# An attention and mixture-of-experts kernel: tile 0 head pair by head pair, two more value buffers, and 14 result tiles held on chip

## The chip, the cores and the metric

One NeuronCore of a Trainium2 chip. The metric is device time of one execution in microseconds (us), as the median of several runs. Matrix products run on TensorE (PE), row reductions and most element-wise work on VectorE (DVE), exponentials and scaled copies on ScalarE (ACT), a few copies and all gathers and scatters on GpSimd (POOL); the plain DMA transfers are issued by SyncE (SP), in program order.

## The reference

Two layers, one after the other, in float32.

1. Attention: q, k, v of shape 4 x 8 x 768 x 64 (batch, heads, sequence, width). Each query attends to the keys nearer than 16 positions and, beside them, to 24 summary keys: the maxima of k over blocks of 32 positions, with log(32) added to the scaled score; the summary values are the means of v over those blocks. One softmax goes over both parts.
2. Mixture of experts: the attention result as 3072 rows of 512. Noisy gates choose two of 8 experts for a row; each chosen expert gives relu(x w1) w2 (512 to 1024 to 512), weighted by the softmax of the two gate values, and the two are added.

## The kernel before

**Attention.** The 3072 rows are 24 tiles of 128 queries, 6 tiles a batch. Heads are held in 4 pairs (`HP`). A tile has 96 local and 24 summary keys for each half of 64 queries. For tile t the work is: `mask_sums` (mask into PSUM), `scores` (32 products), `smax` (row maxima on VectorE), `sexp` (8 exponentials on ScalarE), `p_trans` (8 transposes, copied out by ScalarE), `av` (32 products with the values, into the one PSUM buffer "o"), `norm` (VectorE divides by the sums and writes the result tile X[t]; this empties "o"), `x_pe` and `x_copy` (transpose for the gates), and `x_out` (one DMA of 256 KB writes X[t] to the scratch array `xd` in memory, from where the experts gather rows).

**Order.** It is written out by hand. A loop over steps t = -2 .. 22 issues in step t: the query load of tile t + 5, `norm` of tile t - 1, mask and scores of tile t + 2, its maxima, the transposes of tile t + 1, the exponentials of tile t + 2, the products with the values of tile t, then the transposes of tile t - 1, the second value load of tile t + 3 (`v_load`) and the write of tile t - 2. `at(t, f)` hangs extra pieces into a step: `run(t + 0.1)` and the like call them at fixed places of step t. Each engine runs its own part of this order strictly in sequence, so a piece that waits holds up what stands behind it on its engine.

**Keys.** `KB` holds the keys of a batch (two buffers); `KX` (three buffers) holds for a tile the local keys and the 24 maxima (`kx_local`, `kx_sum`). For batch 0 the keys come as four loads, one a head pair, and `k_head` takes the maxima; for later batches `load_k` brings three tiles' keys (768 KB) and `k_piece` takes the maxima on VectorE, for batch 1 in steps 1 to 3 (two pieces a step), for batch 2 from step 3 on.

**Values.** `VE` holds 128 rows of values a tile, `VD` the 96 rows that its second half of queries needs: three buffers a batch parity, used in turn, so `v_load(3)` waits until tile 0 has been multiplied. Rows 96 to 119 of `VE` and 0 to 23 of `VD` are the 24 block means, from `v_sums` (48 products, four VectorE copies, then GpSimd copies) and `v_rest` (a DMA for the remaining tiles).

**Start.** 100 products of the identity (`warm_up`, line 246) run on TensorE while the first loads come. The loads are queued as: query tile 0, the four key heads, query tile 1, six value tiles, query tile 2, further value and query tiles, gate weights and noise, query tile 4, then batch 1's keys in steps -1 and 0.

**Result tiles.** X[t] has five buffers; tile t is written to `xd` in step t + 2. In step 20 the tokens of tiles 0 to 11 that go to expert 0 are gathered from `xd` (`x_gather`, line 791).

**Experts.** After the attention come the 8 experts in order of their load, mostly dense products on TensorE (lines 854, 909, 1357, 1429), with gathers and scatters on GpSimd. Their buffers for expert 0 (the weights `WT[0]`, the transposed tokens `XTE[0]`) are not in use before step 20, apart from the w1 halves.

Of the kernel before, what the change touches and what calls it, by code (L numbers as in the profile page):

```python
# [8 lines left out]
F32 = mybir.dt.float32  # L9
# [5 lines left out]
OP = mybir.AluOpType  # L15
# [24 lines left out]
QN = 3  # L40
QBUF = 5
QA = 5
WARM = 100
SK = HP * NK
SW = 16 * (D + 1)
NCH = 7
# [17 lines left out]
def attn_moe(ctx, tc, qt, kt, vt, wgn, noise, w1, w2, out):  # L64
# [44 lines left out]
    def load_q(t):  # L109
        QR[t] = QT[t % QBUF]  # L110
        b, j = divmod(t, TS)
        nc.sync.dma_start(QR[t].rearrange("p h b q -> p (h b q)"), qt[b, j])

    def kx_local(t):
        b, j = divmod(t, TS)
        k = KB[b % 2][:, :, j * P:j * P + 64 + W]
        n = HP // 2 if t < 1 else HP
        for h in range(0, HP, n):
            for blk in range(2):
                x, y = KX[t % QN][:, h:h + n, blk, L0[blk]:L0[blk] + W], k[:, h:h + n, 64 * blk:64 * blk + W]  # L120
                if t < 2:
                    nc.scalar.activation(x, y, AF.Copy)
                else:
                    nc.gpsimd.tensor_copy(x, y)

    def kx_sum(t):
        b, j = divmod(t, TS)
        if j < QN:
            x = KX[t % QN].rearrange("p h b k -> p h (b k)")[:, :, W:W + 2 * NB]
            (nc.gpsimd if b else nc.vector).tensor_copy(x.rearrange("p h (b n) -> p h b n", b=2),  # L130
                                                        KM[b][:, :, None, :].to_broadcast([P, HP, 2, NB]))

    def q_piece(t):
        kx_local(t)
        kx_sum(t)

    flat = [x.rearrange("p f n -> p (f n)").bitcast(F32) for x in HT]
    VE = [flat[0][:, :TS * VB].rearrange("p (j c) -> p j c", j=TS), keep.tile([P, TS, VB], F32, name="ve")]
    VD = [[flat[1][:, VB * j:VB * (j + 1)] for j in range(3)],
          [keep.tile([P, VB], F32, name=f"vd{j}") for j in range(2)] + [flat[1][:, 3 * VB:4 * VB]]]  # L140

    def load_ve(b, j):
        nc.sync.dma_start(VE[b % 2][:, j].rearrange("p (h d) -> p h d", h=H), vt[b, j * P:(j + 1) * P])

    load_q(0)
    for h in range(HP):
        nc.sync.dma_start(KB[0][:, h, PAD:PAD + S], kt[0, :, h])


    ji = HT[1].rearrange("p f n -> p (f n)").bitcast(I32)[:, SW:SW + P]  # L150
    nc.gpsimd.iota(ji, pattern=[[1, P]], base=0, channel_multiplier=-1)
# [82 lines left out]
    def k_head(h):  # L234
        if h == 0:
            KM[0] = work.tile([P, HP, NB], F32, name="kmax")
        nc.vector.tensor_reduce(KM[0][:, h], KB[0][:, h, PAD:PAD + S].rearrange("p (n i) -> p n i", i=BLK),
                                axis=AX.X, op=OP.max)

    VO = []  # L240

# [8 lines left out]
    def v_sums(b):  # L250
        if b:
            pt = psum.tile([P, HP, P], F32, name="pt", bufs=2).rearrange("p a b -> p (a b)")
        else:
            pt = psum.tile([P, 2, 512], F32, name="o")[:, 0]
        for j in range(TS):
            for g in range(4):
                nc.tensor.matmul(pt[32 * g:32 * g + NB, 0:C4], ind[:, j, :], VE[b % 2][:, j, C4 * g:C4 * g + C4],
                                 start=(j == 0), stop=(j == TS - 1), skip_group_check=True)
        x, y = VE[b % 2][W:W + NB], [z[0:NB] for z in VD[b % 2]]
        for g in range(4):  # L260
            i, o = pt[32 * g:32 * g + NB, 0:C4], slice(C4 * g, C4 * g + C4)
            if b == 3 and g % 2:
                nc.scalar.activation(x[:, 0, o], i, AF.Copy)
            elif b:
                nc.vector.tensor_copy(x[:, 0, o], i)
            else:
                nc.vector.tensor_copy(x[:, 0, o], i)
        if b == 1:
            nc.gpsimd.tensor_copy(y[0], x[:, 0])
        if b == 0:  # L270
            for i in range(4):
                if i:
                    nc.gpsimd.tensor_copy(x[:, i], x[:, 0])
                if i < 3:
                    nc.gpsimd.tensor_copy(y[i], x[:, 0])

    def v_rest(b):
        x = VE[b % 2][W:W + NB]
        j = 1 if b else 4
        nc.sync.dma_start(x[:, j:], x[:, 0, None, :].to_broadcast([NB, TS - j, VB]))  # L280
        if b:
            for y in VD[b % 2][b == 1:]:
                nc.sync.dma_start(y[0:NB], x[:, 0])

    VX = {}

    def v_load(t):
        b, j = divmod(t, TS)
        y = VD[b % 2][j % 3].rearrange("p (h d) -> p h d", h=H)
        nc.sync.dma_start(y[NB:NB + VR], vt[b, P * j + 64:P * j + 64 + VR])  # L290
        VX[t] = [VE[b % 2][:, j].rearrange("p (h d) -> p h d", h=H), y]

# [16 lines left out]
                                 m[r, None, :].to_broadcast([64, HP, W]), start=True, stop=False,  # L309
                                 skip_group_check=True)  # L310

    def scores(t):
        s, q, k = SC[t], QR[t], KX[t % QN]
        for hp in range(HP):
            for blk in range(2):
                for a in range(2):
                    d = slice(64 * a, 64 * a + 64)
                    nc.tensor.matmul(s[64 * blk:64 * blk + 64, a, hp, :], q[d, hp, blk], k[d, hp, blk, :], start=False,  # L318
                                     stop=hp == HP - 1, skip_group_check=True)
# [16 lines left out]
    def p_trans(t, a):  # L336
        pt = psum.tile([P, HP, P], F32, name="pt", bufs=2)
        for hp in range(HP):
            if t == 0:
                warm_up(1 if a + hp else 8)  # L340
            nc.tensor.transpose(pt[:NK, hp, :], PE_[t][:, a, hp, :], ident)  # L341
        if a == 0:
            PT[t] = awork.tile([P, 2, HP, P], F32, name="pts")
        nc.scalar.activation(PT[t][:NK, a], pt[:NK], AF.Copy)
# [11 lines left out]
                                 start=True, stop=True, skip_group_check=True)  # L356

    xd_w = []

    def norm(t, fill=None):  # L360
        o = PO[t][:, :, :4 * (D + 1)].rearrange("p g (h c) -> p g h c", c=D + 1)
        r = work.tile([P, 2, 4], F32, name="r")
        nc.vector.tensor_scalar(r, o[:, :, :, D], 1e-9, 1.0 / XS, op0=OP.add, op1=OP.mult)
        if fill:
            fill()
        ri = work.tile([P, 2, 4], F32, name="ri")
        nc.vector.reciprocal(ri, r)
        X[t] = work.tile([P, DM], F32, name="x", bufs=5)
        nc.vector.tensor_tensor(X[t].rearrange("p (g h c) -> p g h c", g=2, h=4), o[:, :, :, 0:D],
                                ri[:, :, :, None].to_broadcast([P, 2, 4, D]), op=OP.mult)  # L370

# [419 lines left out]
    def x_gather(e, c, rows=N):  # L791
        if c >= chunks(e):
            return
        if c == 0 and e != 1:
            XTE[e] = (late[0] if e % 2 else moe).tile([P, 2 * DC, CAP], F16, name="xte")
        n = min(P, CAPS[e] - c * P)
        x = XG[gi[0] % len(XG)]
        gi[0] += 1
        r = indirect(
            out=x[:n].bitcast(F32), out_offset=None, in_=xd[:rows],  # L800
            in_offset=bass.IndirectOffsetOnAxis(ap=tb_of(e, c)[:n, 0:1], axis=0),
            bounds_check=rows - 1, oob_is_err=False)
        XC[e, c] = x
        return r
# [162 lines left out]

    warm_up(WARM)
    load_q(1)
    for j in range(TS):  # L970
        load_ve(0, j)
    load_q(2)
    v_load(0)
    v_load(1)
    load_q(3)
    v_load(2)
    nc.sync.dma_start(wg32, wgn)
    nc.sync.dma_start(noi, noise)
    load_q(4)
    for h in range(HP):  # L980
        k_head(h)
    q_piece(0)
    q_piece(1)
    at(-0.9, v_sums, 0)
    at(0.8, v_rest, 0)

    w_alloc(0)
    W0 = [8, 10, 12, 14]
    for i in range(4):
        at(W0[i], w_load, 0, i)  # L990
# [69 lines left out]
    for t in range(-2, NT - 1):  # L1060
        if QBUF <= t + QA < NT:
            load_q(t + QA)
        u = t + 3
        if t >= 1:
            norm(t - 1, (lambda: kx_sum(u)) if u < NT and u != TS else None)
        run(t + 0.02)
        run(t + 0.03)
        if t + 2 < NT:
            mask_sums(t + 2)
            scores(t + 2)  # L1070
        if t == -1:
            q_piece(2)
            q_piece(3)
        run(t + 0.5)
        if t + 2 < NT:
            smax(t + 2)
        if 0 <= t + 1 < NT:
            p_trans(t + 1, 0)
            p_trans(t + 1, 1)
        if t + 2 < NT:  # L1080
            sexp(t + 2, (0, 1) if t + 3 < NT else (0,))
        if u < NT and t >= 1:
            kx_local(u)
        run(t + 0.1)
        if u == TS:
            kx_sum(u)
        run(t + 0.2)
        if t >= 0:
            av_space(t)
        if t + 3 == NT:  # L1090
            sexp(t + 2, (1,))
        if t >= 0:
            av(t)
        run(t + 0.3)
        run(t + 0.31)
        if t >= 1:
            x_pe(t - 1)
        run(t + 0.4)
        if t >= 1:
            x_copy(t - 1)  # L1100
        run(t)
        run(t + 0.8)
        run(t + 0.9)
        if 0 <= t and t + 3 < NT:
            v_load(t + 3)
        if t >= 2:
            x_out(t - 2)

    norm(NT - 2)
# [594 lines left out]
```

## Time and profile before

| | |
|---|---|
| median of 3 runs | 644.94 us (644.83 to 646.68) |
| span of the profiled execution (first to last instruction) | 642.7 us |
| its own time beside the span | not listed apart; the median is 2.24 us above the span |
| TensorE busy | 621.8 us (97%) |
| VectorE, ScalarE, GpSimd busy | 481.6, 316.0, 249.0 us |
| moved by DMA | 127.91 MB, mean 199 GB/s |
| attention stage | about the first 131 us |

The profile is one execution. Its views: the page (busy shares, the span in 40 slices, the costliest groups), the chain of work that ended last, waits by engine, timelines of one engine, and a table by stretches. A releaser "issue" means that the engine waited for nothing that the profile shows.

### The profile page before, as it was taken

The numbers are of one execution on the slowest core, as the hardware profiler recorded it, in microseconds if no ns is written. First come the engines' busy times: TensorE is split into PE (matmuls) and PEld (weight loads), VectorE is DVE, ScalarE is ACT, GpSimd is POOL, SyncE is SP. The second block draws the span as 40 slices with busy tenths as digits, with TensorE's granted clock in tenths as the row PEclk, the third lists the DMA queues.
The fourth block names the chain that finished last, engine by engine and source line by source line (L and its number), as shares of the span: only waits on it lengthen the run. The fifth ranks groups of instructions, "written<-read, shape, count | busy, mean of one in ns | idle before, by whom it ended". The sixth has DMA issues, their size and how long they took to land.

```text
span 642.7 us, 14142 instructions
## 1 busy us (share of the span) xinstructions
PE 621.8 (97%) x5295; PEld 360.3 (56%) x5295; DVE 481.6 (75%) x1039; ACT 316.0 (49%) x692; POOL 249.0 (39%) x432
## 2 busy tenths in 40 slices
PE   8899899899999999999999999999999999999995
PEld 7678777765554554555455544554554455445542
DVE  5848899889797599178878887987898679757510
ACT  4958898852153463065337534654464255425300
POOL 4433044203254433623573256336632542333041
PEclk9989999999999999999999999999999999999999
DMA  9999996678469696636986688779786868763021
GB/s 308 296 294 327 296 303 211 214 265 288 139 200 187 188 221 152 256 91 162 203 245 162 150 212 261 169 139 220 220 199 157 217 202 165 180 193 120 3 95 50
DMA packets 123707, 127.91 MB, mean 199 GB/s; under 512 B 83242, under 2 KB 86674, under 8 KB 123630
## 3 DMA queue, kind: packets, MB, share of 16 engines
q1 hardware_dynamic: 111838, 90.66, 52.9%
q0 software_dynamic: 11792, 36.27, 17.9%
q8 instruction: 43, 0.70, 0.4%
q14 instruction: 34, 0.28, 0.1%
HBM read 81.85 MB, written 25.61 MB: 167 GB/s over the span
## 4 chain that ended last, share of the span: by engine, by line
PE 78%; DVE 11%; ACT 3%; issue 3%; DMA 3%; POOL 0%; POOLq 0%; SPq 0%; DVEq 0%; ACTq 0%
PE pt L1429 29%; PE h L1357 16%; PE h L854 8%; PE pt L909 7%; PE pt L1357 3%; PE o L1357 3%; PE h L909 2%; DVE nm L325 2%; DMA htl<-in_vt_dram 2%; ACT p L333 2%; PE pt L341 1%; PE o L354 1%; PE o L246 1%; PE s L318 1%; DVE y L920 1%
## 5 line engine op out<-in xcount | busy, mean ns | idle before, releaser
L90 POOL DMA_INDIRECT out_dram<-y,tb x52 | 69.3, 1333 | 167.5 <-DVE y L931 129.3
L90 POOL DMA_INDIRECT xg<-xd,tb x54 | 60.4, 1119 | 118.9 <-DVE dsc L653 32.9
L1429 PEld LDWEIGHTS <-hth 128*128 128x128 f16 x576 | 56.4, 98 | 66.7
L931 DVE SCALAR_TENSOR_TENSOR y<-pt,tb,prev 128x512 f32<-128x512 f32 x42 | 31.5, 749 | 65.7 <-PE pt L1429 54.2
L1357 PEld LDWEIGHTS <-w1h 128*128 128x128 f16 x504 | 48.9, 98 | 38.1 <-issue 4.1
L1429 PE MATMUL pt<-w2h,hth 128*128 128x512 f16 x288 | 69.0, 379 | 0.0
L1429 PE MATMUL pt<-w2l,hth 128*128 128x512 f16 x288 | 69.0, 379 | 0.0
L1429 PE MATMUL pt<-w2h,htl 128*128 128x512 f16 x288 | 69.0, 379 | 0.0
L1357 PEld LDWEIGHTS <-w1l 128*128 128x128 f16 x504 | 49.3, 98 | 34.9
L90 POOL DMA_INDIRECT prev<-out_dram,tb x45 | 52.1, 1158 | 24.6 <-issue 12.9
L333 ACT ACTIVATE p<-s,nm 128x120 f32<-128x120 f32 x192 | 50.8, 376 | 0.8
L854 PE MATMUL h<-xte,w1h 128*128 128x384 f16 (+2 forms) x248 | 48.9, 336 | 0.0
L1429 PEld LDWEIGHTS <-htl 128*128 128x128 f16 x288 | 28.2, 98 | 34.0
L1346 ACT ACTIVATE w1h<-stg 128x768 f16<-128x768 f32 (+1 forms) x24 | 22.7, 944 | 40.2 <-DVE stg L1337 40.2
L1389 ACT ACTIVATE hth<-h 128x384 f16<-128x384 f32 (+4 forms) x48 | 23.8, 496 | 35.6 <-PE h L1357 35.6
L1346 ACT ACTIVATE w1l<-stg 128x768 f16<-128x768 f32 (+1 forms) x24 | 22.5, 942 | 37.3 <-DVE stg L1337 37.3
L1357 PE MATMUL h<-xte,w1h 128*128 128x384 f16 (+4 forms) x180 | 39.7, 329 | 0.7 <-DVE h L1383 0.4
L1357 PE MATMUL h<-xte,w1l 128*128 128x384 f16 (+4 forms) x180 | 39.7, 329 | 0.0
L1310 ACT ACTIVATE x<-xt 128x512 f16<-128x512 f32 (+2 forms) x44 | 26.5, 626 | 23.2 <-issue 19.1
L1337 DVE TENSOR_TENSOR stg<-stg 128x256 f32<-128x256 f32 x96 | 36.3, 419 | 0.8
L854 PEld LDWEIGHTS <-w1h 128*128 128x128 f16 x256 | 24.7, 98 | 19.4 <-issue 1.0
L1392 DVE SCALAR_TENSOR_TENSOR htl<-h,hth 128x384 f16<-128x384 f32 (+4 forms) x48 | 26.4, 563 | 11.8 <-ACT hth L1389 11.5
(301 smaller groups left out, 1297.3 us busy)
## 6 DMA issues: line engine op xcount, KB each, us to landing
stg<-in_w_dram SPq DMA_DIRECT2D x64, 512.0 KB
q<-in_qt_dram SPq DMA_DIRECT2D x24, 256.0 KB
xd<-x SPq DMA_DIRECT2D x24, 256.0 KB
out_dram<-xg SPq DMA_DIRECT2D x8, 768.0 KB
kb<-in_kt_dram SPq DMA_DIRECT2D x6, 768.0 KB
hth<-in_vt_dram SPq DMA_DIRECT2D x12, 260.0 KB
htl<-in_vt_dram SPq DMA_DIRECT2D x16, 195.0 KB
ve<-in_vt_dram SPq DMA_DIRECT2D x12, 260.0 KB
```

The lines of the kernel that those rows point to most:

```text
L90: return nc.gpsimd.indirect_dma_start(**kw)
L333: nc.scalar.activation(PE_[t][:, a, hp, :], SC[t][:, a, hp, :], AF.Exp, bias=NM[t][:, 1, a, hp:hp + 1], scale=0.125)
L854: nc.tensor.matmul(ph[:, :n], w1_of(w, wn, c, f), x[:, xo + c, c0:c1], start=(k == 0), stop=(k == 11))
L909: nc.tensor.matmul(py, hx[:, f, c * P:c * P + P], wv[:, f, :], start=st, stop=sp)
L931: nc.vector.scalar_tensor_tensor(y, py[:, :d], gw, pv[:, :d], op0=OP.mult, op1=OP.add)
L1310: nc.scalar.activation(t[:r, c:c + k], src, AF.Copy)
L1337: nc.vector.tensor_tensor(o, x, y, op=op)
L1346: nc.scalar.activation(hi, x, AF.Copy, scale=W1S)
L1357: nc.tensor.matmul(ph[:, :h], w[:, la, a, P * j:P * j + P], x[:, j, :h], start=start and k == 0, stop=k == 5, skip_group_check=True)
L1389: nc.scalar.activation(hh[:, f, t], src, AF.Relu)
L1392: nc.vector.scalar_tensor_tensor(hl[:, f, t], src, 0.0, hh[:, f, t], op0=OP.max, op1=OP.subtract)
L1429: nc.tensor.matmul(py, x, wv[:, f, :], start=st, stop=sp, skip_group_check=True)
```

## The change

- The keys of batch 0 are loaded as heads 0 and 1, query tile 0, head 2, and head 3 in two halves. Tile 0 is worked head pair by head pair (`start`): maxima of the keys and their copy, local keys on ScalarE, scores, 6 warm-up products after each of the first three, then the row maximum and the two exponentials of the head pair before. `WARM` falls from 100 to 48, the 15 warm-up products among tile 0's transposes go, and 12 stand in step 0 after the scores. Local keys of tile 1 move from ScalarE to GpSimd, and the copies of the maxima of tiles 1 and 2 from VectorE to GpSimd.
- `v_sums(0)` moves from step -1 to step 0, behind tile 1's transposes and ahead of tile 0's products with the values. Query tile 2 is loaded ahead of the value tiles.
- Batch 0's second value tile has five buffers (batch 2 still uses three of them); `v_load(3)` and `v_load(4)` are issued in the first queue, behind query tile 4, and no longer in steps 0 and 1. `v_sums(0)` has two more GpSimd copies.
- The result tiles 0 to 13 are written into expert 0's buffers (four in w2h, four in w2l, six in XTE[0]), and their DMAs to `xd` are issued in steps 13 to 19, two a step. Tiles 14 on are written as before.

```diff
-WARM = 100
+WARM = 48
...
-    VD = [[flat[1][:, VB * j:VB * (j + 1)] for j in range(3)],
+    VD = [[flat[1][:, VB * j:VB * (j + 1)] for j in (0, 1, 2, 4, 5)],
...
+    VN = (5, 3, 3, 3)
...
-    load_q(0)
     for h in range(HP):
-        nc.sync.dma_start(KB[0][:, h, PAD:PAD + S], kt[0, :, h])
+        if h == 2:
+            load_q(0)
+        for c in ((0, S // 2), (S // 2, S)) if h == HP - 1 else ((0, S),):
+            nc.sync.dma_start(KB[0][:, h, PAD + c[0]:PAD + c[1]], kt[0, :, h, c[0]:c[1]])
...
+    def start_head(h):
+        k_head(h)
+        for blk in range(2):
+            nc.scalar.activation(KX[0][:, h, blk, L0[blk]:L0[blk] + W], KB[0][:, h, 64 * blk:64 * blk + W], AF.Copy)
+        if h == 0:
+            mask_sums(0)
+        scores(0, h, h + 1)
+        if h < HP - 1:
+            warm_up(6)
+        if h:
+            start_max(h - 1)
+
+    def start_max(h):
+        nc.vector.tensor_reduce(NM[0][:, 0, :, h], SC[0][:, :, h], axis=AX.X, op=OP.max)
+        nc.scalar.activation(NM[0][:, 1, :, h], NM[0][:, 0, :, h], AF.Copy, scale=-0.125)
+        for a in range(2):
+            nc.scalar.activation(PE_[0][:, a, h, :], SC[0][:, a, h, :], AF.Exp, bias=NM[0][:, 1, a, h:h + 1],
+                                 scale=0.125)
...
-        y = VD[b % 2][j % 3].rearrange("p (h d) -> p h d", h=H)
+        y = VD[b % 2][j % VN[b]].rearrange("p (h d) -> p h d", h=H)
...
-            if t == 0:
-                warm_up(1 if a + hp else 8)
...
-        X[t] = work.tile([P, DM], F32, name="x", bufs=5)
+        X[t] = XS_[t] if t < len(XS_) else work.tile([P, DM], F32, name="x", bufs=5)
...
     load_q(1)
+    load_q(2)
     for j in range(TS):
         load_ve(0, j)
-    load_q(2)
     v_load(0)
+    load_q(3)
     v_load(1)
-    load_q(3)
     v_load(2)
     nc.sync.dma_start(wg32, wgn)
     nc.sync.dma_start(noi, noise)
     load_q(4)
...
+    v_load(3)
+    v_load(4)
+    at(0.1, v_sums, 0)
     at(0.8, v_rest, 0)
...
+    XTE[0] = moe.tile([P, 2 * DC, CAP], F16, name="xte")
+    for x in (WT[0]["w2h"], WT[0]["w2l"], XTE[0]):
+        x = x.rearrange("p a b -> p (a b)").bitcast(F32)
+        for i in range(x.shape[1] // DM):
+            XS_.append(x[:, DM * i:DM * i + DM])
+    for t in range(len(XS_)):
+        at(13 + t // 2, lambda t: x_out(t), t)
...
+        if t == 0:
+            warm_up(12)
...
-        if 0 <= t and t + 3 < NT:
+        if 0 <= t < NT - 3 and t + 3 > 4:
             v_load(t + 3)
-        if t >= 2:
+        if t - 2 >= len(XS_):
             x_out(t - 2)
```

## Rows read from the trace of the kernel before

**Rows 1.** Table by stretches: busy time of PE, PEld, DVE, ACT, POOL, clock, DMA, GB/s

```profile
16.00:30.00 14.00, 13.69 (x282) 11.17 (x278) 11.09 (x22) 12.94 (x43) 6.44 (x12) 1.00 1.01 300
30.00:37.00 7.00, 4.75 (x74) 4.06 (x75) 3.72 (x9) 3.21 (x11) 1.53 (x4) 0.76 1.06 284
64.00:92.00 28.00, 25.75 (x527) 20.74 (x519) 25.20 (x84) 24.09 (x78) 8.57 (x14) 1.00 1.00 316
92.00:120.00 28.00, 25.49 (x556) 21.09 (x560) 26.59 (x96) 24.47 (x77) 7.34 (x14) 1.00 0.61 190
```

**Rows 2.** Chain of waits, first 62 us: start, us, what

```profile
21.79 10.41 DMA htl<-in_vt_dram
32.25 1.93 PE o L354 x30
...
36.61 1.02 PE pt L341 x8
37.63 1.08 PE o L354 x32
...
39.30 1.46 PE pt L257 x48
...
41.05 0.82 PE s L318 x32
...
42.35 0.90 issue
...
44.00 1.08 PE o L354 x32
```

**Rows 3.** Timeline of SP's queue, 19 to 41 us: start, us, what it issues

```profile
19.07 1.29 SPq L107 DMA_DIRECT2D kb<-in_kt_dram  x2
...
27.33 0.33 SPq L290 DMA_DIRECT2D htl<-in_vt_dram  x1
30.97 0.34 SPq L112 DMA_DIRECT2D q<-in_qt_dram  x1
...
32.43 0.56 SPq L290 DMA_DIRECT2D htl<-in_vt_dram  x1
...
40.87 1.27 SPq L290 DMA_DIRECT2D vd<-in_vt_dram  x1
```

**Rows 4.** Timelines of VectorE and GpSimd, 27 to 32 us

```profile
27.29 0.69 DVE L231 TENSOR_REDUCE kmax<-kb 128x16 f32<-128x512 f32 x1 [1.26 <-DMA kb<-in_kt_dram]
...
28.93 1.15 DVE L325 TENSOR_REDUCE nm<-s 128x8 f32<-128x960 f32 x1
29.99 2.46 DVE L231 TENSOR_REDUCE kmax<-kb 128x16 f32<-128x512 f32 x4
...
31.32 0.64 POOL L130 COPY kx<-kmax 128x192 f32<-128x192 f32 x2 [7.22 <-DVE kmax L231]
```

**Rows 5.** Timeline of all engines, 6 to 18 us: tile 0

```profile
6.09 2.91 DVE L237 TENSOR_REDUCE kmax<-kb 128x24 f32<-128x768 f32 x3 [0.39 <-DMA kb<-in_kt_dram]
...
11.96 2.12 ACT L333 ACTIVATE p<-s,nm 128x120 f32<-128x120 f32 x8
...
14.39 1.53 PE L257 MATMUL o<-hth 128*24 128x130 f32 x48
...
15.99 1.21 DVE L267 COPY hth<-o 24x130 f32<-24x130 f32 x4 [3.07 <-PE o L257]
...
17.32 0.62 POOL L275 COPY htl<-hth 24x520 f32<-24x520 f32 x1 [5.79 <-issue]
```

**Rows 6.** Line 246 (warm-up), 1.5 to 4.5 us and 6 to 9 us: ns min/median/max

```profile
L246 PE MATMUL o<-identb x28: 289/314/314, 1.5 to 4.4; 128*128 128x128 bf16 x28
...
L246 PE MATMUL o<-identb x53: 219/219/219, 5.8 to 8.7; 128*128 128x128 bf16 x53
```

**Rows 7.** Chain of waits, 62 to 140 us

```profile
66.33 1.63 issue
```

More of the change, by code (lines that the diff above doesn't have):

```diff
@@ L116, in kx_local @@
         k = KB[b % 2][:, :, j * P:j * P + 64 + W]
[L117 to L124, printed above, removed]
+        for blk in range(2):
+            nc.gpsimd.tensor_copy(KX[t % QN][:, :, blk, L0[blk]:L0[blk] + W], k[:, :, 64 * blk:64 * blk + W])
     def kx_sum(t):
@@ L129, in kx_sum @@
             x = KX[t % QN].rearrange("p h b k -> p h (b k)")[:, :, W:W + 2 * NB]
-            (nc.gpsimd if b else nc.vector).tensor_copy(x.rearrange("p h (b n) -> p h b n", b=2),
+            (nc.gpsimd if t else nc.vector).tensor_copy(x.rearrange("p h (b n) -> p h b n", b=2),
                                                         KM[b][:, :, None, :].to_broadcast([P, HP, 2, NB]))
@@ L236, in k_head, with start @@
             KM[0] = work.tile([P, HP, NB], F32, name="kmax")
-        nc.vector.tensor_reduce(KM[0][:, h], KB[0][:, h, PAD:PAD + S].rearrange("p (n i) -> p n i", i=BLK),
-                                axis=AX.X, op=OP.max)
+        for n in ((0, NB // 2), (NB // 2, NB)) if h == HP - 1 else ((0, NB),):
+            nc.vector.tensor_reduce(
+                KM[0][:, h, n[0]:n[1]],
+                KB[0][:, h, PAD + BLK * n[0]:PAD + BLK * n[1]].rearrange("p (n i) -> p n i", i=BLK),
+                axis=AX.X, op=OP.max)
+        x = KX[0][:, h].rearrange("p b k -> p (b k)")[:, W:W + 2 * NB]
+        nc.vector.tensor_copy(x.rearrange("p (b n) -> p b n", b=2), KM[0][:, h, None, :].to_broadcast([P, 2, NB]))
+    def start_head(h):
+        k_head(h)
+        for blk in range(2):
+            nc.scalar.activation(KX[0][:, h, blk, L0[blk]:L0[blk] + W], KB[0][:, h, 64 * blk:64 * blk + W], AF.Copy)
[12 more added lines that the diff above has]
+                                 scale=0.125)
+    def start():
+        NM[0] = work.tile([P, 2, 2, HP], F32, name="nm", bufs=2)
+        PE_[0] = awork.tile([P, 2, HP, NK], F32, name="p")
+        for h in range(HP):
+            start_head(h)
+        start_max(HP - 1)
+        q_piece(1)
     VO = []
@@ L258, in v_sums @@
                                  start=(j == 0), stop=(j == TS - 1), skip_group_check=True)
-        x, y = VE[b % 2][W:W + NB], [z[0:NB] for z in VD[b % 2]]
+        x, y = VE[b % 2][W:W + NB], [z[0:NB] for z in VD[b % 2][:VN[b]]]
         for g in range(4):
@@ L270, in v_sums @@
         if b == 0:
-            for i in range(4):
-                if i:
+            for i in range(VN[0]):
+                if 0 < i < 4:
                     nc.gpsimd.tensor_copy(x[:, i], x[:, 0])
-                if i < 3:
-                    nc.gpsimd.tensor_copy(y[i], x[:, 0])
+                nc.gpsimd.tensor_copy(y[i], x[:, 0])
     def v_rest(b):
@@ L281, in v_rest @@
         if b:
-            for y in VD[b % 2][b == 1:]:
+            for y in VD[b % 2][b == 1:VN[b]]:
                 nc.sync.dma_start(y[0:NB], x[:, 0])
@@ L310, in mask_sums, with scores @@
                                  skip_group_check=True)
-    def scores(t):
+    def scores(t, h0=0, h1=HP):
         s, q, k = SC[t], QR[t], KX[t % QN]
-        for hp in range(HP):
+        for hp in range(h0, h1):
             for blk in range(2):
@@ L358, in attn_moe @@
     xd_w = []
+    XS_ = []
     def norm(t, fill=None):
@@ L793, in x_gather @@
             return
-        if c == 0 and e != 1:
+        if c == 0 and e > 1:
             XTE[e] = (late[0] if e % 2 else moe).tile([P, 2 * DC, CAP], F16, name="xte")
@@ L979, in attn_moe @@
     load_q(4)
[L980 to L984, printed above, removed]
+    v_load(3)
+    v_load(4)
+    at(0.1, v_sums, 0)
     at(0.8, v_rest, 0)
     w_alloc(0)
+    XTE[0] = moe.tile([P, 2 * DC, CAP], F16, name="xte")
[5 more added lines that the diff above has]
+        at(13 + t // 2, lambda t: x_out(t), t)
     W0 = [8, 10, 12, 14]
@@ L1067, in attn_moe @@
         run(t + 0.03)
-        if t + 2 < NT:
+        if t == -2:
+            start()
+        elif t + 2 < NT:
             mask_sums(t + 2)
@@ L1074, in attn_moe @@
         run(t + 0.5)
-        if t + 2 < NT:
+        if t == 0:
+            warm_up(12)
+        if -2 < t < NT - 2:
             smax(t + 2)
@@ L1079, in attn_moe @@
             p_trans(t + 1, 1)
-        if t + 2 < NT:
+        if -2 < t < NT - 2:
             sexp(t + 2, (0, 1) if t + 3 < NT else (0,))
```

## The prediction

> **What bounds the kernel now.** I read the slices of the page first: TensorE is busy nearly everywhere, but the DMA row shows full tenths for the first 92 us only. The table by stretches says the same in numbers: from 16 to 30 us and from 64 to 92 us the DMA engines are full (share 1.01 and 1.00) at 300 and 316 GB/s, from 92 to 120 us they are at 0.61 [rows 1]. So I read the chain of waits of the first 62 us next. It is TensorE work except for one long piece: a value load ("htl") issued at 21.79 us that lands 10.41 us later, at 32.2 [rows 2]. That is the second value tile of tile 3. It is asked for only when tile 0 has left its buffer (three buffers), and by then it queues behind a dozen others. TensorE waits for it 2.28 us, and then the granted clock falls: the mean from 30 to 37 us is 0.76 [rows 1], and the 30 products of tile 3 take 1.93 us where a whole set of 32 takes 1.08 [rows 2].
>
> The SP queue shows why it lands so late. At most eight transfers are on their way: one is issued when the eighth before it has landed. Two loads show it: the value load at 27.33 follows the landing of the key piece issued at 19.07, the query load at 30.97 that of the next key piece [rows 3]. VectorE tells the same from the other end: its maximum over the second key piece waits until 27.29 [rows 4]. The early stage is thus bound by the order and the number of bytes in one full queue, and the question for each edit is what it puts ahead of what.
>
> **Two value tiles moved ahead.** With five buffers the loads for tiles 3 and 4 need no buffer to come free, and stand right behind the fifth query tile, ahead of batch 1's keys. The wait at 29.9 goes: they land some 10 us before their use. But 2 x 195 KB = 0.39 MB now stand ahead of the key pieces, at 300 GB/s 1.3 us. Bounds: 0 (if gaps in the queue hide them) and 2.0 us (at 190 GB/s, the slowest stretch of rows 1); I take 1.3, the rate of the stretch itself. What is late next is VectorE's maximum over the second key piece: 27.29 + 1.3 = 28.6. It stands in order before the normalisation of tile 2, which empties the only "o" buffer that tile 3's products need. From the start of that maximum to the end of the normalisation (the next "nm") are 28.93 - 27.29 = 1.64 us [rows 4], so tile 3's products start at 30.2 and end 1.08 later at 31.3. Before they ended at 32.25 + 1.93 = 34.18 [rows 2]: 2.9 us gained here (bounds 2.2 to 4.2), and with TensorE waiting some 0.6 us, not 2.3, I count no fall of the clock.
>
> **Does it last?** Tile 6 (batch 1's first) needs the maxima: from "nm" to GpSimd's copy are 31.32 - 28.93 = 2.39 us, the copy takes half of 0.64 [rows 4], so scores of tile 6 start at 30.2 + 2.39 + 0.32 = 32.9 and end 0.82 later at 33.7; before at 36.61. The maxima of batch 2's first piece follow (it landed at 30.97 [rows 3], now 32.3, in time): the four maxima end 3.52 us after "nm" (28.93 to 29.99 + 2.46), at 33.7; the next normalisation takes about 1.04, so tile 4's products run from 34.8 to 35.9, before to 38.71. Its value load is there since long. The transposes (39.30 - 38.71 = 0.59) and batch 1's value sums (1.46) end at 37.95, before at 40.76: 2.8. Mask and scores (0.29 + 0.82) and tile 6's transposes (1.02) end at 40.1. Tile 5's value load was issued at 32.43 and landed by 40.87, when the eighth after it could go [rows 3]; the two moved tiles were ahead of it in both orders, so it lands then again. Tile 5's products start at 40.9, before at 44.00 [rows 2], where they had also waited 0.90 us that the chain calls "issue". That is 3.1 us, and from here the chain of before is compute (TensorE, ScalarE, VectorE), not loads: 3.1 us stay to the end.
>
> **Tile 0 by head pairs.** The same 1.8 MB (four key heads, one query tile) must land first, so the last key head comes at about 8 us as before; its three last reductions ended at 9.0 [rows 5]. What followed one after the other (all scores, one maximum of 1.16 us, eight exponentials) is now done per head while keys land. For the last head remain half a reduction (0.48), a copy, 8 of 32 score products, a quarter maximum, two exponentials of 0.27: the exponentials end at about 11, before 14.08 (11.96 + 2.12). But the value sums of batch 0 move behind tile 1's transposes. Tile 1's exponentials can't start before tile 0's transposed copies, about 12.5, and take 2.12, so the sums start near 14.7, before 14.39; then 1.53, the four copies 1.21, GpSimd's first copy 0.62 [rows 5]: tile 0's products start at about 18.1, before at 17.98. Gain 0. Bounds: 2.7 us earlier, 1 us later; neither reaches the end, since VectorE idles 1.26 us before the key piece [rows 4], now about 2.5. The two more GpSimd copies (0.62 each) come after those that tiles 0 to 3 need.
>
> **Warm-up.** 52 of 100 leading matmuls go. The first 28 take 0.104 us each from one to the next (28 in 2.9 us), the later ones 0.055 (53 in 2.9 us) [rows 6]. 48 therefore last until about 6 us, past the rise, and 18 more stand between the heads, 12 before tile 1's transposes. I count 0; below nothing (a gain) is excluded, since they fill waiting time. [...]
>
> **14 results kept on chip.** Steps 2 to 15 lose one write of 0.262 MB each, 0.83 us of queue at 316 GB/s, 11.6 us in all. In the chain after 44 us no load is late, so this gains nothing itself; it keeps the loads ahead of steps that run 3.1 us earlier. In steps 13 to 19 stand 14 writes, 11 more than are taken out there: 9.1 us at 316 GB/s, while 39% of 28 us, 10.9 us, are free [rows 1]. SP issues one in about 0.4 us, 3 in a step of 5 us, ahead of that step's value load, which is three tiles early. Cost 0; without that cover see the third case. The buffers are weights' and expert 0's tiles, first needed in step 20.
>
> **Sum.** 642.7 us of span - 3.1 = 639.6. The median of the runs, 644.94, lies 2.24 above the span: 641.8.
>
> **Rivals.**
> 1. *641.8 as above*, own range 640.7 to 643.2 from the bounds 2.2 to 4.2. For it: each step from a row. Chance 0.47.
> 2. *More is freed: 640.2.* The chain has 1.63 us of "issue" in the middle of tile 12's scores [rows 7], in a stretch with full DMA. If emptier queues end it, the gain is 4.7. For: it falls where the queue is full, as the 0.90 did. Against: the stretch may stay nearly full. Chance 0.25.
> 3. *The late writes take it back: 643.9.* At 190 GB/s the 11 writes need 15.2 us, 4.3 more than is free; the rows of expert 0 that are gathered in step 20 come from these writes. Half of it, 2.1 us, would be the price. It decides if tile 11's write lands after the gather's turn. For: three writes a step, in one ordered queue. Against: share 0.61. Chance 0.19.
> 4. [...] Chance 0.09.
>
> **How the numbers follow.** About 0.3% (1.9 us) is what a measurement tells from no change: faster means below 643.0. The second case and nearly all of the first: 0.70. Same: the rest of the first and most of the third, 0.20. Slower: the fourth and the third's tail, 0.10. The range 639.2 to 644.6 runs from 1 us below the second case to the third with its dearer half, and leaves out the fourth.
>
> **What would show it.** In the changed trace the chain has no 10 us value load and no clock under 1 around 32 us; tile 0's products start within 1 us of 18; VectorE waits for the second key piece until 28 to 29; tile 5's products start near 41; the MoE starts 3 us earlier. Wrong if tile 3's products start after 31.5, if another load takes the stall's place before 60 us, if VectorE's steps after 70 us grow, or if the gathers of step 20 wait for writes.

## The result, and the profile after

The change makes the kernel slower: 650.68 us median (647.55 to 652.46, 7 runs) against 645.34 (643.09 to 646.89, 7 runs); ratio 1.0087, 95% interval 1.0062 to 1.0112, so 4.0 to 7.2 us. The forecast was 641.8, and 650.68 lies outside its range. The profiled execution has a span of 650.0 us and a time of its own of 651.86.

The table by stretches of the changed kernel, same stretches as [rows 1] and, below the dots, 22 to 30 us, in which tile 0's products begin (columns as there):

```profile
16.00:30.00 14.00, 12.05 (x217) 9.57 (x216) 5.93 (x13) 8.45 (x29) 6.80 (x13) 0.88 1.07 328
30.00:37.00 7.00, 6.18 (x126) 5.03 (x125) 4.69 (x9) 5.52 (x19) 0.82 (x2) 1.00 1.06 334
64.00:92.00 28.00, 26.91 (x569) 22.00 (x565) 25.67 (x82) 23.75 (x76) 8.41 (x15) 1.00 0.97 293
92.00:120.00 28.00, 25.33 (x551) 21.13 (x549) 26.70 (x94) 24.83 (x80) 9.99 (x18) 1.00 0.81 268
...
22.00:30.00 8.00, 6.79 (x111) 5.76 (x112) 4.29 (x11) 2.52 (x9) 6.80 (x13) 0.79 1.06 358
```

The stall around 30 us is gone, but VectorE works 5.93 us between 16 and 30 us where it worked 11.09, and the granted clock's mean is 0.79 between 22 and 30. It is 0.50 for 3.4 us of these 8 (24.5 to 27.9) and 1.00 for the rest.

The chain of waits of the changed kernel, 8 to 36 us (start, us, what):

```profile
8.50 0.42 DVE nm L255
...
8.95 0.21 ACT nm L256
...
9.19 0.61 ACT p L258 x2
9.80 0.35 ACT kx L245 x2
10.15 0.49 PE s L346 x8
...
10.74 0.42 DVE nm L255
...
13.02 0.42 DVE nm L255
...
22.84 0.62 POOL htl L303
...
23.51 1.19 PE o L380 x30
...
25.16 1.60 PE s L346 x32
26.76 1.58 PE pt L367 x8
...
35.11 0.82 issue
```

Row maxima of successive heads (each a head pair) start at 8.50, 10.74 and 13.02: one head takes 2.24 to 2.28 us. The steps between the first two are all on the chain: maximum 0.42, scaled copy 0.21, two exponentials 0.61, local keys of the head after next 0.35, scores 0.49, with 0.16 of handing over. From 14.59 to 22.84 the chain has only GpSimd waiting; the timeline below shows what ran there. Tile 0's 30 products start at 23.51; before, its products started at 17.98:

```profile
17.98 0.27 PE L354 MATMUL o<-hth,pts 120*64 120x65 f32 x1
```

At the granted clock of 0.50 the 32 scores of the changed kernel then take 1.60 us, and the transposes, at 0.50 for most of it, 1.58; [rows 2] have 0.82 and 1.02 for them, at 1.00.

The timeline of the changed kernel where tile 0 becomes late:

```profile
10.14 0.47 PE L346 MATMUL s<-kx,q 64*64 64x120 f32 x8 [1.26 <-ACT kx L245]
...
10.74 0.41 DVE L255 TENSOR_REDUCE nm<-s 128x2 f32<-128x240 f32 x1 [0.74 <-PE s L346]
...
15.03 0.61 ACT L258 ACTIVATE p<-s,nm 128x120 f32<-128x120 f32 x2
...
17.02 2.12 ACT L361 ACTIVATE p<-s,nm 128x120 f32<-128x120 f32 x8
...
17.92 1.59 PE L367 MATMUL pt<-ident,p 128*120 128x128 f32 x8
...
19.44 0.73 PE L286 MATMUL o<-hth 128*24 128x130 f32 x17
...
20.37 1.08 PE L286 MATMUL o<-hth 128*24 128x130 f32 x31 [0.19 <-issue]
...
21.51 1.21 DVE L296 COPY hth<-o 24x130 f32<-24x130 f32 x4 [2.91 <-PE o L286]
```

Tile 0's exponentials end at 15.64 (15.03 + 0.61), against 14.08 in [rows 5]. Behind them come tile 1's exponentials, its transposes and only then the value sums, which began at 14.39 in [rows 5] and begin at 19.44 now.

One link of the loop is a wait that the computation does not need. The maximum at 10.74 is that of the second head, whose scores were done by 8.5; it starts when the third head's scores, which stand ahead of it in the program and write the same tile `s`, have ended (0.74 <-PE s).

**How far each tile is late.** Start of the normalisation in the trace, in us against the first profile of the kernel before (19.18 for tile 0, 132.30 for tile 23):

| tile | after | start alone (e2) | buffers + kept (e1) | buffers alone (e12) | kept alone (e13) | before, second profile (e10) |
|---|---|---|---|---|---|---|
| 0 | +5.56 | +4.78 | +0.38 | +0.30 | +0.75 | +0.31 |
| 4 | +5.26 | +2.26 | -2.19 | -2.89 | -0.41 | -1.99 |
| 5 | +4.58 | +1.58 | +0.32 | -2.46 | +2.36 | -2.67 |
| 13 | +3.44 | +1.49 | -2.01 | -2.72 | +0.50 | -4.71 |
| 20 | +3.45 | +1.69 | -1.59 | -2.72 | +0.09 | -4.01 |
| 23 | +4.43 | +2.47 | -0.69 | -1.82 | +1.02 | -3.06 |

The last column is the same program as the reference column: two executions of one program lie 2 to 5 us apart from tile 4 on. Single profiles show mechanisms here; for sizes only the medians count.

### The profile page after: what moved, and what is told of

Read it like the earlier page. It is cut to its first block, busy times and chain, and to the rows that moved or that the text cites. A ratio compares the mean times of both kernels' runs of the same rounds, so it can differ in the third digit from the quotient of the medians.

```text
span 650.0 us, 14074 instructions
## 1 busy us (share of the span) xinstructions
PE 622.9 (96%) x5258; PEld 360.0 (55%) x5258; DVE 482.3 (74%) x1044; ACT 316.5 (49%) x697; POOL 252.3 (39%) x438
## 4 chain that ended last, share of the span: by engine, by line
PE 81%; DVE 8%; ACT 4%; issue 3%; DMA 2%; SPq 1%; POOL 0%; POOLq 0%; DVEq 0%; ACTq 0%
PE pt L1465 28%; PE h L1393 16%; PE h L881 10%; PE pt L936 7%; PE pt L1393 3%; PE o L1393 3%; PE h L936 2%; PE o L380 2%; PE pt L367 2%; PE s L346 1%; ACT p L361 1%; DMA q<-in_qt_dram 1%; DVE htl L1428 1%; PE pt L405 1%; PE o L275 1%
## 5 line engine op out<-in xcount | busy, mean ns | idle before, releaser
L361 ACT ACTIVATE p<-s,nm 128x120 f32<-128x120 f32 x184 | 48.7, 376 | 0.8
```

The source lines that it names most:

```text
L361: nc.scalar.activation(PE_[t][:, a, hp, :], SC[t][:, a, hp, :], AF.Exp, bias=NM[t][:, 1, a, hp:hp + 1], scale=0.125)
```

## The experiments

Unless said otherwise, ratios are to the kernel before on the same chip, with their 95% intervals.

**e1: all but the new start.**

```diff
 (kernel before)
+    VN = (5, 3, 3, 3)          # five second value tiles for batch 0
...
+        X[t] = XS_[t] if t < len(XS_) else work.tile([P, DM], F32, name="x", bufs=5)
```

> Kernel before with the five value buffers and the 14 kept results, without the new start of tile 0 (old load order, 100 warm-up products, value sums behind tile 0's transposes). Theory A (the new start alone costs: its heads run as a loop across ScalarE, TensorE and VectorE, so that tile 0's products with the values start at 22.8 us, not 18.0): those products start at 18.0 again, tile 3's at about 30.2, the time is about 3 us under before, ratio 0.993 to 0.998. Rival B (the late writes or the kept results cost, in steps 13 to 19): ratio 1.003 or more, with longer steps after 80 us.

Measured 646.07 us, ratio 1.0014 (0.9989 to 1.0039), between what the two theories expected. Without the start most of the loss is gone (up to 2.5 us are not excluded), and so is the forecast gain. The chain of e1 shows where the gain went (tile 4 is 2.19 us early, tile 5 no longer):

```profile
39.68 0.47 PE pt L342 x3
40.15 1.94 issue
42.09 1.32 PE pt L342 x5
43.41 1.93 PE o L355 x32
```

TensorE stands 1.94 us in the middle of tile 6's transposes, waiting for nothing that the profile shows, and after it the granted clock's mean is 0.75 (40 to 44 us) and 0.82 (44 to 48), and 32 products take 1.93 us, not 1.08. Counted in the trace, the instruction that waits is TensorE's number 1474. The long pauses of before stand at 1474 (0.89 us) and 2498 (1.63), of after at 962 (0.81), 1218 (1.12) and 2242 (0.85): all are 194 + 256 k; such numbers are called edges here. The page of e1 has a queue that it names after instructions:

```profile
q8 instruction: 43, 0.70, 0.5%
```

These are 43 packets of 16 KB, about one for each 256 of TensorE's 10,700 instructions. A packet starts only after TensorE has crossed an edge, mostly 2 to 6 us after while the DMA share is near 1 (in before and after, up to 60 us: 0.6 to 6.3); from a pause TensorE goes on 1.2 to 1.6 us after the packet has ended, so it pauses where it reaches the next edge sooner. No packet names its engine: that they carry blocks of 256 of TensorE's instructions is not shown directly, it is read from these counts and times.

**e2: the new start alone.**

```diff
 (changed kernel)
-    VN = (5, 3, 3, 3)
+    VN = (3, 3, 3, 3)          # loads 3 and 4 in steps 0 and 1 again
...
-        X[t] = XS_[t] if t < len(XS_) else work.tile(...)
+        X[t] = work.tile([P, DM], F32, name="x", bufs=5)
```

> The new start of tile 0 alone: three value buffers, results written in the step order of before. Theory A: tile 0's products with the values start at 22 to 23 us and the time is over before by 4 to 6 us or more, since tile 3's value load still waits for tile 0's buffer: ratio 1.006 to 1.012. Rival B: ratio 1.000 to 1.003.

Measured 647.75 us, ratio 1.0033 (1.0014 to 1.0051): the start alone costs 0.9 to 3.3 us, less than the 4 to 6 expected. Tile 0 is 4.78 late; what is left at tile 5, 1.58, is less because before, in its first profile, waits in between for its value load (2.28) and at instruction 1474 (0.89).

**e3: local keys of all heads ahead of the head loop.**

```diff
 (changed kernel, start)
+        for h in range(HP):
+            for blk in range(2):
+                nc.scalar.activation(KX[0][:, h, blk, ...], KB[0][:, h, ...], AF.Copy)
         for h in range(HP):
             start_head(h)      # without these copies
```

> The changed kernel with one move: ScalarE copies the local keys of all four head pairs before the first exponential, so that no copy stands behind the exponentials of the head pair before. Theory A, with ScalarE's order as what closes the loop: the exponentials of tile 0 end at about 13, not 15.6, tile 0's products with the values start at about 20, not 22.8, and the time falls by 2 to 3 us against the changed kernel: ratio to before 1.002 to 1.006. Rival C (the loop is VectorE's, whose key maxima stand behind the row maxima of the head pair before, or the loads'): the exponentials end later than 14.5 and the time stays, ratio 1.007 or more.

Measured 648.91 us, ratio 1.0059 (1.0030 to 1.0088), tile 0 5.76 late. The theory that ScalarE's copies make the loop slow falls as the only cause. The timeline of e3 has the same period, through VectorE:

```profile
10.30 0.41 DVE L253 TENSOR_REDUCE nm<-s 128x2 f32<-128x240 f32 x1 [0.71 <-PE s L347]
10.62 1.00 DVE L235 TENSOR_REDUCE kmax<-kb 128x12 f32<-128x384 f32 x2
...
11.66 0.19 DVE L240 COPY kx<-kmax 128x48 f32<-128x48 f32 x1
...
12.00 0.43 PE L347 MATMUL s<-kx,q 64*64 64x120 f32 x8 [1.39 <-DVE kx L240]
...
12.58 0.41 DVE L253 TENSOR_REDUCE nm<-s 128x2 f32<-128x240 f32 x1 [0.73 <-PE s L347]
```

A later head's key maxima and their copy stand in VectorE's order behind this row maximum, and that head's scores wait for them (12.00): 10.30 to 12.58 is again 2.28 us. Two engines close the same loop, and both ways pass through the same wait: here too a maximum starts at the end of the next head's scores. No run took that wait away.

**e4: as e3, and the value sums back in step -1.**

```diff
 (e3)
-    at(0.1, v_sums, 0)
+    at(-0.9, v_sums, 0)
...
-        if t == 0:
-            warm_up(12)
```

> As the run with all local keys first, and the value sums of batch 0 back behind tile 0's transposes (step -1), where before had them; the 12 warm-up products of step 0 go with it, since they write the same buffer. Theory A: tile 0's products with the values start near 18, 2 us earlier than with the sums behind tile 1's transposes, and the time is 1 to 3 us under before: ratio 0.995 to 0.999. Rival D (the place of the sums costs nothing, since the loads hold everything): same start of the products as in the run with all local keys first, within 0.5 us, and the same ratio.

Measured 646.84 us, ratio 1.0021 (1.0004 to 1.0038), not below 1 as expected. Tile 0 is 3.39 late, 2.4 less than in e3, with a pause of 1.60 us at instruction 450 ahead of it; the clock stays at 1.00 from 16 to 30 us.

**e5 and e6: the edges moved.** In e1 (e5) and in the kernel before (e6), 72 warm-up products of 128 columns become 18 of 512: 108 TensorE instructions fewer, about the same TensorE time (in before a product of 128 columns follows the last after 0.055 us [rows 6], one of 512, line 1429, after 0.216).

```diff
-    warm_up(WARM)
+    warm_up(28)
+    warm_wide(18)      # identity times four copies of it, 512 columns
```

> The buffers and the kept results without the new start (as the first experiment), but the last 72 of the 100 leading warm-up products are 18 of 512 columns: the same TensorE time with 108 TensorE instructions fewer. Fetch theory (TensorE gets its instructions in blocks of 256 through the DMA engines, and pauses where the next block isn't there when the full queue delays it): the 1.94 us pause that stood at TensorE instruction 1474, in tile 6's transposes at 40.15 us, is gone from there; pauses stand again at instruction 194 + 256 k, now 108 instructions later in the work: about 0.7 us near 30 us and 0.3 to 0.7 near 44 us. Tile 5's normalisation starts 1 to 2 us before that of the kernel before instead of 0.3 after it. Median 643.0 to 645.0, 1 to 3 below the first experiment. Rival (the pause belongs to tile 6's transposes, which wait for something that the profile doesn't show): it stays at tile 6's transposes near 40 us, 1.9 us long, and the median stays within 0.7 of 646.1.

> The kernel before with the same shorter list of warm-up products (108 TensorE instructions fewer, the same TensorE time), nothing else. Fetch theory: the pauses of 0.89 us ending at 43.24 and 1.63 us ending at 67.95 leave their places (tile 6's transposes, tile 12's scores); 0.4 to 0.8 us each stand some 108 instructions later, near 45, 63 and 70 us, in all 1.7 to 2.5 us instead of 2.5 to 3; the median is 0 to 1.5 us below the kernel before. Rival (the pauses belong to the work at their places): both stay where they were in the work, and the time is that of before within 0.3%.

Measured: e5 643.7 us, 1.0005 (0.9986 to 1.0024); e6 643.24 us, 0.9994 (0.9973 to 1.0015). The chain of e5:

```profile
23.87 0.28 PE s L314
24.15 1.09 issue
...
31.57 0.26 PE o L360 x3
31.83 0.70 issue
...
37.95 0.56 PE pt L264 x13
38.51 0.52 issue
```

The pause at tile 6's transposes is gone, and pauses stand at instructions 706, 962 and 1218, in other work: they belong to the edges, not to the work at their places. In e6 the pauses are at 706 (0.51), 962 (0.61), 1218 (1.57), 1474 (0.72) and 1986 (0.94). Their sum, 4.4 us, is larger than the 2.5 of the first profile of before, not smaller as expected. Both intervals hold 1: moving the edges moved the pauses, but no change of the time is shown.

**e7: only the sums back in step -1.**

```diff
 (changed kernel)
-    at(0.1, v_sums, 0)
+    at(-0.9, v_sums, 0)
...
-        if t == 0:
-            warm_up(12)
```

> The changed kernel with batch 0's value sums back in step -1 (ahead of tile 1's transposes) and without the 12 warm-up products of step 0; the local keys stay between the heads. If the place of the sums is what makes tile 0's products late: they start near 20.5 instead of 23.5, tile 0's normalisation about 3.4 us after that of before (as with the local keys first as well) instead of 5.6, and the median falls to 646.3 to 647.8. Rival (the serial loop over the four heads is all of it, the sums only fill time in which TensorE waits anyway): the normalisation stays at 5 to 5.6 us late and the median at 649 to 651.

Measured 645.91 us, ratio 1.0047 (1.0030 to 1.0063), below the changed kernel's 1.0087 (1.0062 to 1.0112; the intervals just touch). At tile 0 I missed: 5.20 late, not 3.4. Its chain shows why, a pause of 1.94 us at instruction 450 and slow work behind it (8 transposes in 1.89 us, 1.02 in [rows 2]):

```profile
17.52 0.61 PE s L346 x22
18.13 1.94 issue
20.07 1.06 PE s L346 x10
21.12 1.89 PE pt L367 x8
23.02 1.31 PE o L380 x32
```

**e8: two copies back from GpSimd to VectorE.** The last four microseconds had differed by kernel, not by execution. The scatter's last packet, the end, and GpSimd's long DRAIN behind its last scatter, with the semaphore ahead of it, from the trace:

```
kernel    GpSimd instr.  packet ends  end     semaphore  DRAIN starts  tail
before    759            639.27       642.68  637.54     637.63        3.40
e2        762            642.51       645.91  640.52     640.62        3.40
after     764            645.11       649.99  643.06     645.50        4.89
e7        764            639.05       644.01  637.06     639.52        4.97
e8        762            645.23       648.66  643.03     643.13        3.43
```

```diff
-            (nc.gpsimd if t else nc.vector).tensor_copy(...)
+            (nc.gpsimd if b else nc.vector).tensor_copy(...)
```

> The changed kernel with the two copies of the maxima for tiles 1 and 2 back on VectorE, nothing else: GpSimd has 762 instructions in the trace instead of 764. In the four kernels with 764 GpSimd's last DRAIN starts 2.2 to 2.5 us after the semaphore ahead of it, behind a packet of queue q14 (instructions), and 4.9 to 5.0 us pass from the scatter's last packet to the end; in the five with 759 to 762 it follows at once, and 3.3 to 3.4 us pass. Fetch theory (the last drain stands just behind the edge of a block of GpSimd's instructions): the DRAIN follows at once again, the tail is 3.4 us, and the median falls 1.5 us, to 648.7 to 649.6 if the kernel before is at 645.3. The first tiles change by less than 0.5 us. Rival (the tail belongs to the new start together with the kept results, by what they leave in the queues): tail 4.9 us, and no change of the median.

The tail is 3.43 again: with 764 GpSimd instructions the DRAIN starts 2.4 us after the semaphore ahead of it, with 762 at once. That is 1.5 us of the loss, and all four profiles with 764 have it (tail 4.9 to 5.0), none of the twelve with 759 to 762 (3.3 to 3.5). That GpSimd's list has edges too, with the DRAIN behind one, is argued and not shown: in those four it starts 1.1 to 1.3 us after a packet of the second instruction queue, q14, has ended. Measured 649.58 us, ratio 1.0070 (1.0043 to 1.0096): lower than 1.0087, but the intervals overlap, and I was wrong on the first tiles: tile 0 is 8.27 late. VectorE makes tile 1's copies at 15.20 where GpSimd made them from 12.12 on, and the granted clock is 0.50 from 10.4 to 20.6 us of this execution (mean of the whole 0.987, the lowest of the profiled ones); tile 1's scores, ahead of tile 0's transposes, take 1.88 us instead of 1.03.

**e9: buffers with moved edges, nothing else.**

```diff
 (e5)
-        X[t] = XS_[t] if t < len(XS_) else work.tile(...)
+        X[t] = work.tile([P, DM], F32, name="x", bufs=5)
```

> The kernel before with the five value buffers and the shorter list of warm-up products (108 TensorE instructions fewer), but without the kept results and the new start. If the kept results cost nothing, as the constant distances of tiles 13 to 20 say: the ratio to the kernel before is that of the same with kept results (1.0005 with an interval of 0.9986 to 1.0024), the attention stage ends 2 to 2.4 us before that of the kernel before, the span is near 640.2. Rival (the kept results cost 1 to 2 us in an ordinary execution, by their late writes or the buffers of expert 0 that they hold, and the profiled execution doesn't show it): the ratio is 0.996 to 0.998, a median 1.3 to 2.6 us below the kernel before.

Measured 644.21 us, ratio 0.9984 (0.9960 to 1.0007): not shown to be faster. No version tried was shown to beat the kernel before with the computation whole.

**e10 and e11: the kernel before, and e5, once more.** No edit.

> The kernel before once more, to see how far two profiled executions of one program stand apart on another chip. If the pauses of the instruction fetch are set by the program: the same instruction numbers (1474 and 2498) with pauses within 0.5 us of 0.89 and 1.63, and each tile's normalisation within 0.5 us of the first profile up to tile 23. Rival (they depend on how the transfers of that execution happen to meet): pauses at other of the numbers 194 + 256 k, or of other length by over 0.5 us, and tiles that differ by 1 to 2 us from about 43 us on; the single-profile differences of 1 to 2 us between kernels then say little.

> The kernel of the experiment with moved boundaries once more, in a second profiled execution: its median was 1.7 us above its profiled execution (643.7 and 642.0). If that profile was a lucky one: this one's tiles from 43 us on stand 1 to 2 us later, with longer or more pauses at 194 + 256 k, and its time is 643 to 645. Rival (what is lost in ordinary executions lies outside the attention stage): the tiles stand within 0.5 us of the first profile (-2.4 us to the kernel before at tile 23), and the time is still 643 to 645.

e10: 642.06 us, one run, below the 19 other runs of this kernel on its chip (642.54 to 649.66). The pauses at 1474 and 2498 are absent, and the value load that the forecast was built on costs half as much; from e10's table by stretches and its TensorE timeline:

```profile
30.00:37.00 7.00, 5.63 (x115) 4.75 (x114) 5.01 (x9) 5.61 (x19) 1.54 (x4) 1.00 1.06 325
```

```profile
31.18 0.27 PE L354 MATMUL o<-htl,pts 120*64 120x65 f32 x1 [1.09 <-DMA htl<-in_vt_dram]
```

1.09 us instead of 2.28, and no fall of the clock (1.00, was 0.76). The queue is as full as in the first profile (1.06), yet these pauses are absent: a full queue doesn't always end in a pause. e11: 645.83 us, with pauses of 1.13, 0.87 and 1.59 us at 1218, 2242 and 3010 that the first profile of e5 had shorter or not at all. The edges are the program's; how long TensorE waits at one is the execution's.

**e12 and e13: buffers alone, kept results alone.**

```diff
 (e12: kernel before)
+    VN = (5, 3, 3, 3)
...
 (e13: kernel before)
+        X[t] = XS_[t] if t < len(XS_) else work.tile(...)
```

> The kernel before with the five value buffers alone. If the kept results cost 1 to 2 us in ordinary executions, the buffers alone gain: ratio 0.996 to 0.999 (both together had 1.0014, interval 0.9989 to 1.0039), a median 0.7 to 2.6 us below the kernel before. If they cost nothing: the ratio of both together, 1.000 to 1.002, the gain at tile 4 (2 to 3 us in the trace, no wait for a value load) being lost again in pauses of the instruction fetch.

> The kernel before with the kept results alone (tiles 0 to 13 held in expert 0's buffers, written in steps 13 to 19). If they cost: ratio 1.002 to 1.004, 1.3 to 2.6 us, and the trace shows later gathers in step 20 or later loads of expert 0. If they cost nothing, or gain a little since steps 2 to 15 have one write less in the full queue: ratio 0.998 to 1.001, tiles 13 to 20 at a constant distance from the kernel before.

Measured 644.39 us, 0.9995 (0.9971 to 1.0019), and 644.78 us, 1.0005 (0.9986 to 1.0024). The kept results cost nothing that can be measured (at most 1.5 us by the interval; tiles 13 to 16 stand at a constant +0.50, then +0.1), and the buffers gain nothing that can be. The place where they act went as forecast; VectorE's timeline in e12, then its table by stretches:

```profile
28.23 0.69 DVE L233 TENSOR_REDUCE kmax<-kb 128x16 f32<-128x512 f32 x1 [1.25 <-DMA kb<-in_kt_dram]
...
29.87 1.15 DVE L326 TENSOR_REDUCE nm<-s 128x8 f32<-128x960 f32 x1
```

```profile
30.00:37.00 7.00, 6.36 (x141) 5.31 (x144) 6.02 (x10) 5.94 (x19) 1.54 (x4) 1.00 1.06 359
```

The second key maximum waits for its keys until 28.23 (forecast 28.6), the next row maximum starts at 29.87 (forecast 30.2), and the clock stays at 1.00.

**e14: less in the queue.** This kernel leaves out the second value loads and computes with other values in their place.

```diff
 (e13)
-        nc.sync.dma_start(y[NB:NB + VR], vt[b, P * j + 64:P * j + 64 + VR])
-        VX[t] = [VE[b % 2][:, j]..., y]
+        VX[t] = [VE[b % 2][:, j]...] * 2
```

> The kernel with the kept results alone, without the second value loads: the second half of a tile's queries uses the first half's value rows, so that part of the attention is left out, 195 KB a tile; TensorE's instructions are the same in number and place. With the writes of tiles 0 to 13 in steps 13 to 19 about 0.45 of 1.1 MB a tile is missing from the queue up to step 13. Theory (the full queue makes the instruction blocks late): the packets start within 2.5 us after TensorE has crossed an edge, instead of 2.5 to 6, and the pauses of 1.19, 0.88 and 2.55 us at instructions 962, 1218 and 1474 are below 0.4 each; no clock below 1.00 from 20 to 92 us; the attention stage ends 3 to 6 us before that of the kept results alone, the median 640 to 642.5. Rival (the block takes its time whatever the queue holds, 5 us or so): pauses of 0.8 us and more at 962, 1218 or 1474 in work that runs at its full pace, and a gain below 2 us.

Measured 641.04 us (640.69 to 641.27, 4 runs), ratio 0.9931 (0.9906 to 0.9956). The long pause in the chain of e13 (instruction 1474), then the tables by stretches, first of e13, then of e14:

```profile
41.94 2.56 issue
```

```profile
30.00:37.00 7.00, 6.03 (x114) 4.83 (x106) 6.23 (x11) 4.62 (x15) 1.54 (x4) 1.00 1.07 289
37.00:64.00 27.00, 24.32 (x526) 19.71 (x524) 16.03 (x51) 19.17 (x62) 9.74 (x19) 0.94 0.94 264
```

```profile
30.00:37.00 7.00, 7.00 (x136) 5.52 (x128) 6.15 (x10) 6.10 (x19) 1.54 (x4) 1.00 0.60 218
37.00:64.00 27.00, 26.55 (x610) 22.02 (x610) 21.20 (x68) 21.73 (x71) 11.42 (x24) 1.00 0.67 214
```

With the DMA share at 0.60 and 0.67 TensorE is busy 7.00 of 7 us. The packet behind the edge at 1218 starts 1.2 us after it (e13: 5.5), and the pause at 1474 is gone; tile 23 is 5.3 us earlier than in e13. Where the queue is still full (share 1.05 from 16 to 30 us) the packets are still 3.5 to 4.5 us late, with a pause of 0.83 us at 706. The 16 traces together say it more surely than this one. Of their 195 edges between 15 and 92 us, 104 had a DMA share of 1.0 or more in the 3 us behind them: the packet started 3.6 us after the edge in the median, and 40 had a pause of over 0.3 us at the next edge. At 24 the share was under 0.8: no packet started later than 2.0 us, and none had a pause at the next edge. So the packets come late where the queue is full, and at e14's shares of 0.60 and 0.67 the pause at 1474 went. The gain of e14 is not all from that: with the second value loads went the waits for them as well (2.28 us in before, 1.09 and 0.86 in e10). The four times lie within 0.6 us, seven of the kernel before on the same chip within 3.0; that the queue makes the spread is likely, but four runs do not show it.

## Why the prediction was wrong

- **The failed step: "Tile 0 by head pairs ... Gain 0. Bounds: 2.7 us earlier, 1 us later; neither reaches the end."** I added the last head's own pieces after the last key load (exponentials end at about 11). They end at 15.64: I had not followed the loop in which each engine's strict order, and a maximum that waits for the next head's scores, tie a head to the heads before it, 2.24 to 2.28 us a head. With the sums behind tile 1's transposes, the whole of it reaches tile 0's products: 23.51 instead of the 18.1 of the forecast, and 4.6 of these 5.4 us come from the exponentials. It does reach the end: e2, 0.9 to 3.3 us.
- **"3.1 us stay to the end" failed too.** The steps up to there held (e12: second key maximum 28.23, tile 4 2.89 us early; e1: 2.19). But it was 2.28 us with a fall of the clock in one execution and 1.09 without in another, and where loads didn't hold TensorE, pauses at edges did (e1 1.94 us, e12 1.33 and 1.35). 3.1 us would be 0.48%; e12's interval ends at 0.29% of gain.
- **"where they had also waited 0.90 us that the chain calls "issue""**: I passed over it as a constant. It stands at an edge, instruction 1474: the packet behind 1218 had started 3.7 us late, and TensorE went on 1.46 us after its end. So does the 1.63 of [rows 7] (2498: 4.8 us late, on 1.22 us after its end). Rival 2 looked in the right place: of 24 edges with a DMA share under 0.8 none had a pause at the next (e14). The change did not empty the queue enough: its share was 1.06 to 1.07 from 16 to 37 us.
- **"I count 0; below nothing (a gain) is excluded"**, on the warm-up: a cost came, though no run shows that the thinner warm-up made it. The granted clock is 0.50 for 3.4 us (24.5 to 27.9) after TensorE's wait of 1.32 us ahead of tile 0's products, for which the sums' new place leaves it no other work; in before it is 0.50 for 3.4 us as well (32.4 to 35.8), after the wait of 2.28, and 1.00 behind the pause of 1.63. The forecast gave its fourth case 0.09. No run shows a price for it beyond these 3.4 us: at 1.93 / 1.08 = 1.8 [rows 2] they cost about 1.5 (an estimate), and the late exponentials come beside them.
- **"The two more GpSimd copies (0.62 each) come after those that tiles 0 to 3 need"** holds, but GpSimd's list is longer with them and the other new copies, and its long DRAIN starts 2.4 us late: 1.5 us at the end (e8).
- **"Cost 0"**, on the 14 results kept on chip, holds (e13), and rival 3 does not.
- **Sum.** Start alone 2.1 us (0.9 to 3.3) and tail 1.5 make 3.6; measured 5.3 (4.0 to 7.2, the medians 650.68 and 645.34). The buffers and the kept results add nothing that can be measured, though e1 leaves room for 2.5 us. The remaining 1.7 lie within the intervals and their cause stays open. Pauses at edges are one candidate, argued and not shown: up to 92 us after pauses for 0.81, 1.12 and 0.85 us, e2 for 0.47 and 1.16. The forecast's last term, 2.24 us from span to median, joined two executions; every run on record lies 1.7 to 1.9 above its own span.

## What to carry to other kernels

Before splitting a stage into parts to overlap it, write the parts down in each engine's own order and follow one part's chain through all engines, with every wait: the period of that loop, not the last part's own work, sets the end. Take a "gap without a cause" seriously, count the instruction at which it falls, and profile the same program twice before a single stall of 2 us becomes a forecast.

## What the runs showed of the hardware

- TensorE's long pauses without a shown cause stand at its instructions 194 + 256 k (before: 0.89 us at 1474, 1.63 at 2498), and the queue named after instructions moves 43 packets of 16 KB beside 10,700 of them. With a DMA share of 1.0 or more the packet started 3.6 us after the edge in the median, and at 40 of 104 such edges a pause of up to 2.55 us followed where TensorE came to the next one; with a share under 0.8 none of 24 did. The count of instructions thus decides where the pauses fall: 108 fewer moved every pause (e5, e6), without a change of the median that could be measured.
- At GpSimd's end two instructions more or less decided over 1.5 us: the tail is 4.9 to 5.0 us with 764, 3.3 to 3.5 with 759 to 762 (e8).
- One program's executions on one chip spread over 6.5 us (before, 29 runs beside e5, 640.82 to 647.28).
